# Block-wise first inversion and a regrouping list scheduler in a fused delta-rule, gated-MLP and rotor kernel

## The chip, the cores and the metric

One core of one Trainium2 chip. The metric is the device time of one execution in microseconds, as the median of several. "Before" took 726.74 us (median of 3, 725.66 to 727.87).

Engines by their names in the profile: PE is TensorE's matmul, PEld its weight load, DVE is VectorE, ACT ScalarE, POOL GpSimd, and SP the engine that starts the DMA transfers.

## The reference

Three layers in a row, all in fp32, with 4 batches, 8 heads, 768 tokens and head dimension 48:

```python
for t in range(S):                      # 1: delta rule, per batch and head
    y[:, :, t] = einsum('bhd,bhde->bhe', q[:, :, t], state)
    v_old = einsum('bhde,bhd->bhe', state, kt)          # kt: normalised key
    state = state + bt * einsum('bhd,bhe->bhde', kt, vt - v_old)
...
h = maximum(x @ w_in, 0); u, v = halves of h            # 2: gated MLP
v_n = (v - mean) / sqrt(var + 1e-6)
gated = u * (w_spatial @ v_n + b_spatial);  x = gated @ w_out
...
theta = x @ w_theta; zr, zi = x * cos(theta), x * sin(theta)   # 3: rotor
u = x + w_tok_r @ zr + w_tok_i @ zi;  out = u + maximum(u @ w_ch, 0)
```

## The kernel before

**Chunks.** The recurrence runs in chunks of 64 tokens. 12 chunks make a batch, 48 in all make the chain (0 to 47), and all 8 heads of a chunk run together, two heads side by side on the partitions. Within a chunk the recurrence is a triangular system. Its matrix is inverted beforehand, for 8 chunks (a "round") at a time, so there are 6 rounds; round 0 stands at the start of the program with nothing to hide it.

For each chunk the chain (`chain`) issues on PE, with the line of the profile:
- L875, the read product: keys with the state. DVE subtracts v (L878).
- L887, the update product: the inverted matrix with that difference. ACT or DVE copy it out of PSUM (to U).
- L900, the state product, copied out to S, on which the next chunk's L875 depends.
- L929, the output products, copied to xs and sent through DRAM to layer 2.

Beside them stand the Gram products (`gram2`, L666: keys with keys, two chunks at a time) and the J products (`jit`, L820: keys with queries).

**The inversion** (`invert`). Each 64-row matrix is split into two 32-row diagonal blocks and the block below. DVE transposes (L704), makes norms and factors, scales (L721), and substitutes: 30 steps, each a multiplication (L743) and an addition (L754) over the remaining columns. In round 0 the columns are split in two interleaved sets, so that four instructions belong to one step. Then it scales again (L757) and transposes twice (L761, L763). PE couples the two blocks in two products of 32 rows (L781, L787), with copies in between.

**Layers 2 and 3** are large matmuls (L1040), each fp32 product split into three. V and U (x with w_in), S (w_spatial) and the w_out, theta, y and w_ch products. V, U and S of the first batches run between the products of the chain. What follows the chain is large matmuls alone. The memory for w_out and theta (`p2a`) opens only when all tasks of layer 1 are done.

**The order** is not written out. `Plan` collects tasks with priorities, estimated durations and dependencies, and lists them at build time: at each step the earliest task, and among tasks that could start at once that of the smallest priority. On PE `pe_pick` may choose a large task instead, to keep the clock up, and `filler` (L545) puts idle transposes into gaps. Each engine then runs its list strictly in order.

```python
end, warm, w, acc = self.pe_run(c[1], c[0], c[2], False)
if w > int(c[0] // HAMW) and not warm:
    return best
```

## Time and profile before

| | |
|---|---|
| median of 3 executions | 726.74 us (725.66 to 727.87) |
| the profiled execution | 725.02 us |
| its span, first to last instruction | 722.9 us |
| PE busy | 675.3 us (93%) |
| DVE busy | 560.8 us (78%) |
| ACT busy | 356.3 us (49%) |
| mean granted PE clock, share of full | 0.981 |
| update product of chunk 0, 8 and 47 starts at | 46.76, 110.10, 373.87 us |

The profile is of one execution, and its times count from the span's start. A busy time is the time in which at least one instruction of the engine ran. "Idle" is the rest. A row of the timeline merges like instructions that follow one another: its first column is the start of the first, its second the time to the end of the last. Durations of single instructions overlap their successors; the price of one in a stream is the time from start to start.

### The profile page before, as it was taken

Reading aid. Unit: us, or ns where it says so; the run is one execution under the profiler, and the core shown is the slowest. Engines: PE = TensorE matmul, PEld = TensorE weight load, DVE = VectorE, ACT = ScalarE, POOL = GpSimd, SP = SyncE. Lnnn points to the kernel's source line nnn. Section 1 sums busy time; section 2 is a strip of 40 time slices with the busy share of each in tenths; the row PEclk is TensorE's granted clock in tenths of the full one; section 3 lists DMA queues with packets and bytes.
Section 4 is the critical chain, followed back from the end, with each engine's and each line's share of the span. In section 5 each row is a group of like instructions: output and inputs, shape, how many; then the busy total and the mean of one; then the engine's idle time right before and its main releaser. Section 6 shows DMA issues by size and latency. Waiting matters only on the chain.

```text
span 722.9 us, 23312 instructions
## 1 busy us (share of the span) xinstructions
PE 675.3 (93%) x9750; PEld 619.1 (86%) x9750; DVE 560.8 (78%) x1603; ACT 356.3 (49%) x877; POOL 12.4 (2%) x22
## 2 busy tenths in 40 slices
PE   4585889899999999999999999999999999999997
PEld 4575567688887788878889999999999999999997
DVE  6999989989999989996767868977466745674555
ACT  5756456553369643278646854743244324431331
POOL 0010010010010010010000000000000000000000
PEclk9995899999999999999999999999999999999999
DMA  8544624534567443666778764521111111111001
GB/s 298 172 111 132 201 76 137 145 87 131 171 199 228 125 118 99 188 195 189 241 217 282 222 210 128 162 74 30 66 29 30 30 66 30 30 40 55 1 1 65
DMA packets 74120, 90.62 MB, mean 125 GB/s; under 512 B 7328, under 2 KB 58912, under 8 KB 74016
## 3 DMA queue, kind: packets, MB, share of 16 engines
q1 hardware_dynamic: 74016, 89.14, 40.3%
q8 instruction: 76, 1.25, 0.7%
q14 instruction: 28, 0.23, 0.1%
HBM read 66.70 MB, written 22.41 MB: 123 GB/s over the span
## 4 chain that ended last, share of the span: by engine, by line
PE 54%; DVE 1%; ACT 0%; issue 0%
PE m L1040 29%; PE y L1040 22%; PE m L1351 1%; PE ru L929 1%; PE ru L887 0%; PE ru L875 0%; PE s L900 0%; PE gp L820 0%; PE gp L781 0%; PE gp L787 0%; DVE bgm L964 0%; DVE ul L971 0%; DVE uf L1427 0%; ACT bgr L513 0%; DVE bgm L962 0%
## 5 line engine op out<-in xcount | busy, mean ns | idle before, releaser
L1040 PE MATMUL m<-w,vh 128*128 128x384 f32 x384 | 102.9, 349 | 0.0
L1040 PE MATMUL y<-wr,xTh 128*128 128x384 f32 x432 | 86.9, 338 | 0.0
L1040 PE MATMUL y<-w,xTl 128*128 128x384 f32 x432 | 85.6, 338 | 0.0
L1040 PEld LDWEIGHTS y<-wr,xTh 128*128 128x128 f32 x432 | 75.9, 188 | 0.0
L1040 PEld LDWEIGHTS y<-w,xTl 128*128 128x128 f32 x432 | 75.4, 188 | 0.0
L1040 PEld LDWEIGHTS m<-w,vh 128*128 128x128 f32 x384 | 66.2, 188 | 2.9
L1040 PE MATMUL m<-w,vl 128*128 128x384 f32 x192 | 64.4, 336 | 0.0
L754 DVE TENSOR_TENSOR un<-un,tmp 128x30 f32<-128x30 f32 (+22 forms) x209 | 60.8, 302 | 1.5
L743 DVE TENSOR_TENSOR tmp<-un 128x30 f32<-128x30 f32 (+23 forms) x209 | 60.5, 301 | 1.5
L1376 DVE TENSOR_SCALAR bgr<-m 128x384 int32<-128x384 f32 x22 | 12.3, 558 | 51.1 <-PE m L1040 50.9
L513 ACT ACTIVATE U<-ru 128x96 f32<-128x96 f32 x76 | 15.2, 250 | 63.6 <-PE ru L887 54.3
L1040 PE MATMUL m<-xTh,wih 128*128 128x256 f32 x144 | 44.9, 312 | 1.5 <-ACT hv L513 1.5
L513 ACT ACTIVATE x<-m 128x384 f32<-128x384 f32 x22 | 10.6, 482 | 70.2 <-PE m L1040 70.2
L1040 PE MATMUL m<-wo,gh 128*128 128x384 f32 x176 | 44.7, 334 | 0.0
L1040 PE MATMUL m<-xTl,wih 128*128 128x256 f32 x144 | 40.6, 282 | 0.0
L1040 PE MATMUL m<-xTh,wil 128*128 128x256 f32 x144 | 40.6, 282 | 0.0
L1040 PE MATMUL m<-uh,wc 128*128 128x384 f32 x144 | 38.2, 335 | 0.0
L513 ACT ACTIVATE bgr<-bgr 128x384 uint8<-128x384 uint8 x34 | 36.6, 1075 | 0.5
L1040 PEld LDWEIGHTS m<-w,vl 128*128 128x128 f32 x192 | 36.0, 188 | 0.0
L1040 PE MATMUL m<-wih,xTh 128*128 128x512 f32 x72 | 32.6, 452 | 3.5 <-DVE jp L826 1.2
L1040 PE MATMUL m<-wt,xh 128*128 128x384 f32 x132 | 33.8, 337 | 0.0
L929 PE MATMUL ru<-jp,U 64*64 64x64 f32 x768 | 33.2, 229 | 0.0
(189 smaller groups left out, 1632.6 us busy)
## 6 DMA issues: line engine op xcount, KB each, us to landing
kq<-in_kqT_dram SPq DMA_DIRECT2D x48, 256.0 KB, 3.8
vk<-in_vkn_dram SPq DMA_DIRECT2D x48, 192.0 KB, 2.9
kg<-in_kgT_dram SPq DMA_DIRECT2D x24, 256.0 KB, 3.7
gd<-gt SPq DMA_DIRECT2D x32, 192.0 KB, 3.0
xd<-xs SPq DMA_DIRECT2D x48, 96.0 KB, 2.8
xr<-xd SPq DMA_DIRECT2D x24, 192.0 KB, 3.6
bgr<-in_w_r_dram SPq DMA_DIRECT2D x12, 384.0 KB, 3.8
bgr<-in_w_i_dram SPq DMA_DIRECT2D x12, 384.0 KB, 4.0
```

What stands on the lines that cost most here:

```text
L513: nc.scalar.activation(out=out, in_=in_, func=func, **kw)
L743: nc.vector.tensor_tensor(out=t3, in0=un.t[:, k:k + 1, 0:k].to_broadcast([128, m, k]), in1=un.t[:, t0:32:st, k:k + 1].to_broadcast([128, m ...
L754: nc.vector.tensor_tensor(out=un.t[:, t0:32:st, 0:k], in0=un.t[:, t0:32:st, 0:k], in1=t3, op=ALU.add)
L929: mm(out=PYv[h]()[o:o + 64, c0:c0 + CH], lhsT=lh, rhs=rh, start=f, stop=w == 1 or UF[hp] > 0, skip_group_check=True)
L1040: mm(out=view(), lhsT=a, rhs=c, start=(start and q == 0 and s_ == 0), stop=(stop and q == tot - 1 and s_ == 2))
L1351: nc.tensor.transpose(v3()[:, kk, :], x2.t[:, kk * 128:(kk + 1) * 128], ident.t)
L1376: P.add(o_dve(DM), lambda e: nc.vector.tensor_scalar(out=ni.t.bitcast(I32), in0=th(), scalar1=1.0 / TWO_PI, scalar2=None, op0=ALU.mult), [ ...
```

## The change

Two things at once.

**The first inversion in 16-row blocks** (round 0 only, `I16 = 1`). After the same transpose and factors, DVE substitutes only in the two 16-row diagonal blocks of each 32-row block, both in one instruction, 14 steps. It zeroes the block between them, scales, and makes two transposes (L774, L776). PE joins the 16-row blocks: product A (L793), a combination on DVE (L812), products B (L799) and C (L805), and copies. Then come the coupling products of before (now L725 and L731, in `couple`), in four groups of 8 matrices. The first two groups have priority over chunk 0, the others are placed among the first chunks. The other five rounds substitute as before, but mask and scale with straight writes in place of strided ones.

**The scheduler.** J, later Gram and output tasks become "lazy" (`LZ`, `LZY`, `LZG`): where the choice falls on one, and the task before was not a read or update product, another task that is ready goes first, unless the lazy one's priority is no larger than that of the last such product. `STAY` goes from 0 to 350: while PE runs small products and a large one would be next, a small one that can start within 350 ns goes first. Large V and S tasks are cut into 3 matmuls in place of 6, and constants of the clock estimate and the priorities of the second inversion change. Random priority offsets (`NUDGE`) go away. New memory for y (always in the `ru` bank) and unpadded S and U follow.

```diff
-FILL_LOW = 0.4
-FILL_K = 4
+FILL_LOW = .5
+FILL_K = 16
...
-PER = 6
+PER = 3
...
+LZ = 0.0
+LZY = 0.0
+LZG = 1
+GAPY = 0
+STAY = 350.0
+NUDGE = ()
+SPER = 3
...
-I1P = -8.0
+I1P = 2.5
...
     def pe_pick(self, l, s0, c):
 
+        if c[1].lazy is not None and not self.gap and c[1].prio > self.prog - c[1].lazy:
+            o = [x for x in l if x[1].lazy is None and x[0] <= s0 + 1.0]
+            if o:
+                c = min(o, key=lambda x: (x[1].prio, x[1].uid))
...
+                self.gap = t.gap
+                if t.gap:
+                    self.prog = t.prio
...
+    def invert16(r, pr, gx, G, gg, un, gt, dg, u3, dv, g2):
...
+        for k in range(14, 0, -1):
+            m = 15 - k
+            tmp = r_tmp.new()
...
+                V.tensor_tensor(out=t4, in0=dv()[:, :, k:k + 1, 0:k].to_broadcast([128, 2, m, k]),
+                                in1=dv()[:, :, k + 1:16, k:k + 1].to_broadcast([128, 2, m, k]), op=ALU.mult)
...
+                V.tensor_tensor(out=dv()[:, :, k + 1:16, 0:k], in0=dv()[:, :, k + 1:16, 0:k], in1=t4, op=ALU.add)
...
+        A([("DVE", 1090.0)], lambda e: V.transpose(out=p1.t.rearrange("p u s -> p s u"), in_=u3()[:, :, 0:16].rearrange("p t s -> p s t")),
+          [un], [p1], pr + 0.05, crit=cr, port=False)
+        A([("DVE", 1944.0)], lambda e: V.transpose(out=zt.t.rearrange("p u t -> p t u"), in_=u3()), [un], [zt], pr + 0.1, crit=cr, port=False)
...
+        for h, u0 in enumerate(range(0, 32, MG)):
+            p2 = pr + 0.2 if cr and h == 0 else 8.0 * r + 2.0 * h - (GH if r else HP0)
...
+            def fA(e, u0=u0, va=va):
+                for u in range(MG):
+                    for q in (0, 32, 64, 96):
+                        mm(out=va()[q:q + 32, u, :], lhsT=gx[q:q + 16, u0 + u, 0:32], rhs=p1.t[q:q + 16, u0 + u, :],
+                           start=True, stop=True, tile_position=(q, q))
+
+            def fB(e, u0=u0, vb=vb, cc=cc, vc=vc):
+                for u in range(MG):
+                    for q in (0, 64):
+                        mm(out=vc()[q:q + 32, u, :], lhsT=zt.t[q:q + 32, u0 + u, :], rhs=cc[q:q + 32, u, :],
+                           start=True, stop=True, tile_position=(q, q))
...
+            A(o_dve(16 * MG), lambda e, cc=cc, va=va: V.scalar_tensor_tensor(
+                out=cc[:, :, 0:16], in0=va(), scalar=mask3.t[:, 32:33],
+                in1=mask3.t[:, 0:16].unsqueeze(1).to_broadcast([128, MG, 16]), op0=ALU.mult, op1=ALU.add),
+              [m, mask3], [cb], p2, crit=cr, port=False)
...
+            couple(r, h, u0, MG, p2 + 0.05, gx, G, lambda u, u0=u0, ux=ux: ux.t[:, u - u0, :], [ux], [bx], [bx, bz], ps, o + 256, m2)
...
             A([("DVE", d_dve(1024))], lambda e: nc.vector.tensor_tensor(
-                out=un.t.rearrange("p t u -> p u t"), in0=gx[:, :, 0:32], in1=mask2.t.unsqueeze(1).to_broadcast([128, 32, 32]), op=ALU.mult),
-              G + [mask2, gg[1], gg[3]], [un], pr)
+                out=gx[:, :, 0:32], in0=gx[:, :, 0:32], in1=mask2.t.unsqueeze(1).to_broadcast([128, 32, 32]), op=ALU.mult),
+              G + [mask2, gg[1], gg[3]], gm2, pr)
...
         A([("DVE", d_dve(1024))], lambda e: nc.vector.tensor_tensor(
-            out=gx[:, :, 0:32].rearrange("p s t -> p t s"), in0=un.t, in1=gt.t.unsqueeze(1).to_broadcast([128, 32, 32]), op=ALU.mult),
-          [un, gt] + ub, gg, pr + 0.05, crit=cr)
+            out=u3(), in0=u3(), in1=gt.t.unsqueeze(1).to_broadcast([128, 32, 32]), op=ALU.mult), [un, gt], ub, pr + 0.05, crit=cr)
...
+        elif LZG:
+            mt.lazy = LZ
...
-        A(o_pe(YPE if c else YPE // 2), fy, [kq, jp] + (ss if c else []) + uu, pys + [(xs, True)], pr + YP, act=0.6)
+        A(o_pe(YPE if c else YPE // 2), fy, [kq, jp] + (ss if c else []) + uu, [py, (xs, True)], pr + 0.5, act=1.0)
         ys_b.append(P.tasks[-1])
+        P.tasks[-1].lazy = LZY
```

**What moves, on DVE at the end of the first inversion** (`un` is the matrix, `tmp` the multiplied row, `GX` the 64-row matrices). Before:

```order
L743 TENSOR_TENSOR tmp<-un 128x42 x2
L754 TENSOR_TENSOR un<-un,tmp 128x14x3 x2
L743 TENSOR_TENSOR tmp<-un 128x28
L743 TENSOR_TENSOR tmp<-un 128x30
L754 TENSOR_TENSOR un<-un,tmp 128x14x2
L754 TENSOR_TENSOR un<-un,tmp 128x15x2
L743 TENSOR_TENSOR tmp<-un 128x15 x2
L754 TENSOR_TENSOR un<-un,tmp 128x15 x2
L757 TENSOR_TENSOR GX_121<-un,gaT 128x32x32
L761 STREAM_TRANSPOSE un<-GX_121 128x32x32
L763 STREAM_TRANSPOSE GX_121<-un 128x32x32
```

Now, at the same place:

```order
L763 TENSOR_TENSOR un<-un,tmp 128x2x12x3
L758 TENSOR_TENSOR tmp<-un 128x52
L763 TENSOR_TENSOR un<-un,tmp 128x2x13x2
L758 TENSOR_TENSOR tmp<-un 128x28
L763 TENSOR_TENSOR un<-un,tmp 128x2x14
L771 TENSOR_TENSOR un<-un,gaT 128x2x16x16
L774 STREAM_TRANSPOSE p_583<-un 128x16x32
L776 STREAM_TRANSPOSE uT<-un 128x32x32
L850 TENSOR_TENSOR GX_123<-GX_123,mask_115 128x32x32
L812 SCALAR_TENSOR_TENSOR cc_152<-gp,mask_116 128x8x16
```

Each step has one multiplication and one addition, where it had two of each; the steps go from 14 down, not from 30. L850, the mask of the second inversion, has come up to stand right behind.

**On PE from the first coupling to the update product of chunk 0** (`un`, `ct`, `cc`, `ux`, `uT`, `p` are inputs of the coupling and the join, `ident` the fillers). Before, from the first L781 on:

```order
L781 MATMUL gp<-un,GX_121 32x32 x16
L545 MATMUL ru<-ident 128x128 x15
L787 MATMUL gp<-GX_121,ct 32x32 x16
L820 MATMUL m<-kq 64x64 x8
L545 MATMUL ru<-ident 128x128 x10
L820 MATMUL m<-kq 64x64 x8
L545 MATMUL gp<-ident 128x128
L781 MATMUL gp<-un,GX_121 32x32 x16
L545 MATMUL ru<-ident 128x128
L887 MATMUL ru<-rt,GX_121 64x48 x8
```

Now, from the first C product to chunk 0's update product (L1029); products A and B of the first group stand right ahead of this piece:

```order
L805 MATMUL gp<-uT,cc_152 32x32 x32
L799 MATMUL gp<-cc_153,uT 32x32 x16
L725 MATMUL gp<-ux,GX_122 32x32 x16
L805 MATMUL gp<-uT,cc_153 32x32 x32
L962 MATMUL m<-kq 64x64 x8
L731 MATMUL gp<-GX_122,ct 32x32 x16
L561 MATMUL ru<-ident 128x128
L725 MATMUL gp<-ux,GX_122 32x32 x16
L561 MATMUL ru<-ident 128x128
L962 MATMUL m<-kq 64x64 x8
L561 MATMUL ru<-ident 128x128 x2
L1029 MATMUL ru<-rt,GX_122 64x48 x8
```

Two rounds through the copies (A to B and C, then the coupling) have taken the place of one, and 4 fillers that of 27.

**On PE around the output product of chunk 47** (`w`, `vh`, `vl` are S, `wih`, `wil`, `xTh`, `xTl` are V). Before, the output product (L929) comes 6 matmuls behind the update product:

```order
L887 MATMUL ru<-rt,GX_123 64x48 x8
L1040 MATMUL m<-w_1260,vh 128x384
L1040 MATMUL m<-w_1419,vh 128x384
L1040 MATMUL m<-w_1260,vl 128x384
L1040 MATMUL m<-w_1503,vh 128x384
L1040 MATMUL m<-w_1511,vh 128x384
L1040 MATMUL m<-w_1503,vl 128x384
L929 MATMUL ru<-kq,S_118 64x64 x2
L929 MATMUL ru<-jp,U_120 64x64 x2
```

Now (L1067) it is preceded by V products, and followed by more of them; the update product lies 189 rows of large matmuls ahead:

```order
L1177 MATMUL m<-wil_158,xTh 128x512
L1177 MATMUL m<-wih_155,xTl 128x512
L1177 MATMUL m<-wih_156,xTh 128x512
L1177 MATMUL m<-wil_159,xTh 128x512
L1177 MATMUL m<-wih_156,xTl 128x512
L1067 MATMUL ru<-kq,S_119 48x64 x2
L1067 MATMUL ru<-jp,U_121 48x64 x2
```

It has moved behind work on other batches, and with it the end of layer 1.

## Rows read from the trace of the kernel before

**Rows 1.** Busy time by stage: start:end, length, busy us (instructions), clock, DMA.

```profile
0.00:40.45 40.45, 23.75 (x469) 22.05 (x470) 34.16 (x148) 23.44 (x53) 0.44 (x8) 1.00 0.63 210
46.76:110.10 63.34, 47.07 (x1333) 38.30 (x1332) 59.06 (x183) 37.57 (x110) 1.93 (x2) 0.81 0.50 146
110.10:373.87 263.77, 253.33 (x5738) 212.59 (x5737) 234.76 (x724) 146.14 (x399) 7.98 (x8) 0.99 0.55 163
373.87:722.90 349.03, 344.81 (x2059) 340.74 (x2058) 227.20 (x536) 146.47 (x311) 0.14 (x2) 1.00 0.27 84
```

**Rows 2.** Timeline of DVE, first inversion: start, us, engine line op.

```profile
9.76 1.92 DVE L704 STREAM_TRANSPOSE un<-GX 128x1024 f32<-128x1024 f32 x1 [0.16 <-ACT GX L513]
...
14.10 1.23 DVE L721 TENSOR_TENSOR un<-un,gaT 128x1024 f32<-128x1024 f32 x1
...
15.62 0.28 DVE L743 TENSOR_TENSOR tmp<-un 128x30 f32<-128x30 f32 x2
...
25.00 0.47 DVE L743 TENSOR_TENSOR tmp<-un 128x120 f32<-128x120 f32 x2
25.39 0.47 DVE L754 TENSOR_TENSOR un<-un,tmp 128x120 f32<-128x120 f32 x2
...
38.95 1.25 DVE L763 STREAM_TRANSPOSE GX<-un 128x1024 f32<-128x1024 f32 x1
```

**Rows 3.** Timeline of DVE, end of the second substitution.

```profile
90.39 0.27 DVE L754 TENSOR_TENSOR un<-un,tmp 128x108 f32<-128x108 f32 x1
90.69 0.24 DVE L743 TENSOR_TENSOR tmp<-un 128x84 f32<-128x84 f32 x1
...
91.90 0.21 DVE L743 TENSOR_TENSOR tmp<-un 128x30 f32<-128x30 f32 x1
92.15 0.22 DVE L754 TENSOR_TENSOR un<-un,tmp 128x30 f32<-128x30 f32 x1
```

**Rows 4.** Groups on DVE by form: busy us, mean ns | idle before.

```profile
L761 DVE STREAM_TRANSPOSE un<-GX 128x1024 f32<-128x1024 f32 x6 | 12.1, 2024 | 0.1
L757 DVE TENSOR_TENSOR GX<-un,gaT 128x1024 f32<-128x1024 f32 x6 | 12.0, 2000 | 0.1
...
L721 DVE TENSOR_TENSOR un<-un,gaT 128x1024 f32<-128x1024 f32 x6 | 7.3, 1218 | 0.1
```

**Rows 5.** Timeline of PE, update, state and output products, first w_out.

```profile
46.76 0.45 PE L887 MATMUL ru<-rt,GX 64*64 64x48 f32 x16
...
110.10 0.45 PE L887 MATMUL ru<-rt,GX 64*64 64x48 f32 x16
...
111.30 0.52 PE L900 MATMUL s<-U,vk 64*48 64x48 f32 x16 [0.51 <-ACT U L513]
...
375.50 0.27 PE L929 MATMUL ru<-kq,S 48*64 48x64 f32 x2
...
396.06 0.51 PE L1040 MATMUL y<-wo,gh 128*128 128x384 f32 x2
```

**Rows 6.** Busy time around the second inversion, and at the lower clock.

```profile
40.20:96.54 56.34, 41.75 (x1101) 34.11 (x1099) 53.86 (x176) 31.44 (x96) 1.89 (x2) 0.79 0.52 154
...
57.00:79.60 22.60, 15.52 (x361) 12.63 (x361) 21.81 (x82) 11.34 (x37) 0.00 (x0) 0.50 0.53 156
```

**Rows 7.** Timeline of PE, from large to small products.

```profile
92.58 0.28 PE L1040 MATMUL m<-xTl,wih 128*128 128x256 f32 x1
92.69 0.28 PE L1040 MATMUL m<-xTh,wil 128*128 128x256 f32 x1
92.90 0.40 PE L900 MATMUL s<-U,vk 64*48 64x48 f32 x16
```

**Rows 8.** Timeline of PE, V products of 512 columns.

```profile
384.21 0.39 PE L1040 MATMUL m<-wih,xTh 128*128 128x512 f32 x1
384.44 0.39 PE L1040 MATMUL m<-wil,xTh 128*128 128x512 f32 x1
```

**Rows 9.** Timeline of DVE, the last part of w_out.

```profile
399.14 0.55 DVE L971 TENSOR_TENSOR wo<-cvm,wo 128x384 fp32r<-128x384 f32 x1
```

More of the change, by code (lines that the diff above doesn't have):

```diff
@@ L114 @@
 WEARLY = 1
+I16 = 1
+BK16 = 12
+MG = 8
+HP0 = 1.8
+GH = 1.0
 SLX = 0.0
@@ L155 @@
 class Task:
-    __slots__ = ("opts", "fn", "deps", "prio", "extra", "crit", "users", "left", "eng", "start", "end", "allocs", "uid", "big", "act", "credit", "order", "banks", "port", "part", "mode", "slack")
+    __slots__ = ("opts", "fn", "deps", "prio", "extra", "crit", "users", "left", "eng", "start", "end", "allocs", "uid", "big", "act", "credit", "order", "banks", "port", "part", "mode", "slack", "lazy", "gap")
 class PEFILL:
@@ L588 @@
     PSb = [Buf(tile_=PSt) for _ in range(2)]
+    r_y, PYv = r_ru, [RUt[:, h, 256:448] for h in range(2)]
+    RUz = Buf(tile_=RUt)
     for b_ in PSb:
@@ L620 @@
     load(mask2, lambda: mask2.t, mask2_c, 16384, -21.2)
+    load(mask3, lambda: mask3.t, mask3_c, 16896, -21.1)
+    CC = [pools["pa"].tile([128, MG, 32], F32, name=f"cc{i}") for i in range(2)]
+    ccb = [Buf(tile_=x) for x in CC]
+    for i in range(2):
+        A([("POOL", 450.0)], lambda e, i=i: nc.gpsimd.tensor_copy(CC[i], mask3.t[:, 0:32].unsqueeze(1).to_broadcast([128, MG, 32])),
+          [mask3], [ccb[i]], -20.0, port=False)
     for q in (32, 96):
         A([("DVE", 300.0)], lambda e, q=q: nc.vector.memset(PSt[q:q + 32, :, 0:2 * D], 0.0), (), PSb, -31, port=False, part=q)
-    for i in range(2):
-        A([("POOL", 100.0)], lambda e, i=i: nc.gpsimd.memset(St[i][:, HP * D:], 0.0), (), SS[i], -30 + i, port=False)
-        A([("POOL", 100.0)], lambda e, i=i: nc.gpsimd.memset(Ut[i][:, HP * D:], 0.0), (), UU[i], -30 + i, port=False)
+        A([("DVE", 600.0)], lambda e, q=q: nc.vector.memset(RUt[q:q + 32, :, 256:448], 0.0), (), [RUz], -31, port=False, part=q)
     kq_b, vk_b, jp_b = {}, {}, {}
@@ L680, in gram2, with couple, f2, f3 @@
                 A(o_cpp(256), lambda e, w=w, gxj=gxj: copy(e, gxj, pvs[w]()), [pss[w]], [G], pr, port=False)
+    def couple(r, h, u0, mu, p2, gx, G, xf, xr, x3, x4, ps=None, o=256, pb=None):
+        cr = r == 0
+        if ps is None:
+            ps = pb = r_gp.new()
+        ct = r_ct.new()
+        pv = GPt[:, o:o + mu * 32].rearrange("p (a b) -> p a b", b=32)
+        def f2(e):
+            for u in range(mu):
+                for q in (0, 64):
+                    mm(out=pv[q + 32:q + 64, u, :], lhsT=gx[q:q + 32, u0 + u, 32:64], rhs=xf(u0 + u)[q:q + 32],
+                       start=True, stop=True, tile_position=(q, q + 32))
+        def f3(e):
+            for u in range(mu):
+                for q in (0, 64):
+                    mm(out=pv[q:q + 32, u, :], lhsT=ct.t[q + 32:q + 64, u, :], rhs=gx[q + 32:q + 64, u0 + u, 32:64],
+                       start=True, stop=True, tile_position=(q + 32, q))
+        A(o_pe(525 * mu // 8), f2, xr + G[u0 // HP:(u0 + mu) // HP], [(ps, True), (pb, pb is ps)], p2, crit=cr, act=0.38, mode=3)
+        P.tasks[-1].order.update(seqs[-1:])
+        seqs.append(P.tasks[-1])
+        for q in (1, 3):
+            A(o_cpp(32 * mu), lambda e, q=q: copy(e, ct.t[32 * q:32 * q + 32, 0:mu], pv[32 * q:32 * q + 32]),
+              [pb], [(ct, True)], p2, crit=cr, port=False, part=32 * q)
+            ps.readers.append(P.tasks[-1])
+        A(o_pe(525 * mu // 8), f3, [ct] + x3, [(ps, True), (pb, True)], p2, crit=cr, act=0.46, mode=3)
+        for q in (0, 2):
+            A(o_cpp(32 * mu), lambda e, q=q: copy(e, gx[32 * q:32 * q + 32, u0:u0 + mu, 32:64], pv[32 * q:32 * q + 32]),
+              [pb] + x4, [G[i] for i in range(u0 // HP, (u0 + mu) // HP)], p2, crit=cr, port=False, part=32 * q)
+            ps.readers.append(P.tasks[-1])
@@ L823, in jit @@
             jp = jp_b[g] = r_jp.new()
-            A(o_pe(JPE), f, [kq_b[g]], pss + [jp], pr, after=grams if r < 2 else (), act=0.55)
+            A(o_pe(JPE), f, [kq_b[g]], pss + [jp], pr, after=grams if r < 2 else (), act=0.75).lazy = LZ
             for h in (0, 1):
@@ L830, in jit @@
             jp = jp_b[g] = jp_b[g + 1] = r_jp.new()
-            A(o_pe(2 * JPE), f, [kq_b[g], kq_b[g + 1]], pss + [jp], pr, after=grams if r < 2 else (), act=0.55)
+            A(o_pe(2 * JPE), f, [kq_b[g], kq_b[g + 1]], pss + [jp], pr, after=grams if r < 2 else (), act=0.75).lazy = LZ
             A(o_dve(512), lambda e: nc.vector.tensor_tensor(
@@ L899, in fs @@
                         i = 64 - a if UF[hp] else a
[L900 removed]
+                        mm(out=at(PSt, SB[hp])[a:a + D], lhsT=v.t[i:i + 64, 1, hp, :], rhs=u[i:i + 64, UB[hp], :],
                            start=f, stop=l, skip_group_check=True)
[L903 removed]
+            A(o_pe(SPE), fs, [v] + uu, PSb, pr, crit=True, act=0.81)
             for h in (0, 1):
[L905 to L911 removed]
+                A(o_cpp(96), lambda e, h=h: copy(e, two(sn)[0:112, h], PSt[0:112, h, 0:2 * D]), [PSb[h]], [ssn[h]], pr, crit=True, port=False)
+        py = r_y.new()
         yc = (lambda w, hp: (w, 64 * (SB[hp] % 2)) if UF[hp] else (YF[hp], 128))
```

190 lines of the change are left out of this document (116 added, 74 removed).

## The prediction

> **What bounds the kernel now.** I read the busy time by stage first, then the timelines of PE and DVE where the stages meet, and the order of the instructions on PE and DVE before and after. A chunk is 64 tokens of one batch, counted 0 to 47; "product 8" is the update product (L887) of chunk 8. Four stages are to be seen in [rows 1]. Until 40.45 us nothing can start, since the first inversion runs on DVE: PE's 23.75 us of busy time there are Gram products and fillers. From product 0 to product 8 (46.76 to 110.1 us, 63.3 us) DVE is the bound: 59.06 busy against PE's 47.07, at a mean clock of 0.81. From product 8 to product 47 (263.8 us) PE is: 253.33 busy, so 10.4 idle. After product 47 PE is alone on the path, 344.81 of 349.03.
>
> So I ask two things: how much earlier product 8 comes, and whether PE has more or less to do after it. By the order, PE has passed the same 63 large matmuls at product 8 before and now, and the same 2745 stand behind it.
>
> **The first inversion.** Before, DVE starts it at 9.76, scales at 14.10, substitutes from 15.62 to about 34.9 in 118 instructions, and ends the last transpose at 40.20 (38.95 + 1.25) [rows 2]. Now only the two 16-row diagonal blocks are substituted, in 28 instructions of 28 to 112 elements, each of which needs the one before it. Before, two interleaved halves of the columns kept the instructions apart: four of 120 elements start 0.39 us per pair, 0.195 each (25.00, 25.39) [rows 2]. The price of dependent ones stands where the second inversion ends: 0.30 us from start to start at 108 elements, 0.25 at 30 [rows 3]. With these 28 instructions cost 14 x 0.26 (28 to 72) + 14 x 0.30 (88 to 112) = 7.8 us. Their bounds are 28 x 0.195 = 5.5 and 28 x 0.30 = 8.4; I take 7.8, since the rows are of this very code. In the Trainium skill, "VectorE: DVE Perf Modes", section "The DRAIN you can't avoid", chained instructions cost no more than unchained ones, because each waits for the pipeline to empty anyway. The rows disagree (0.30 against 0.195 at about the same size); by that rule the substitution would take 5.5, and the forecast would be 2.3 lower.
>
> The rest goes by [rows 2, 4]. From the first transpose to the scaling stays 4.34. Scaling half of the elements: half of 1.22, 0.6, and the diagonal 0.1. Second scaling of the half: 0.6. A transpose that writes with a stride costs 2.02, half of one 1.0, so the two new ones 3.0. Sum: 9.76 + 4.34 + 0.7 + 7.8 + 0.6 + 3.0 = 26.2; with the one instruction of chunk 0 in between (0.3) and handoffs I take 26.9. That is 13.3 us before 40.20.
>
> The join is new: 320 matmuls of 32 rows, 4 combining instructions on DVE and 40 copies out of PSUM of a quarter of the partitions. Half of it stands ahead of product 0, half among chunks 1 to 4. From the end of DVE's part to product 0 it was 6.6 us (40.20 to 46.76) [rows 2, 5]. Now one more round through PE, a copy and PE again stands there: between 6.6 and twice that, product 0 at 33.5 to 40.1. I take 36, nearer to the one round, as the two first groups run into each other.
>
> **From there to product 8.** Chunk 0 early is worth nothing by itself: chunk 8 is the first that needs the second inversion, and that is DVE's. Before, from 40.20 to its last transpose at 96.54 DVE had 56.34 us and was busy for 53.86 of them [rows 6]. By the order it now has 195 instructions between these two marks, and had 175. The second inversion itself gets cheaper: masking and scaling with straight writes, 1.22 each where strided ones took 2.00 [rows 4], while its first transpose now reads across, 1.92 in place of the 1.25 of a straight one [rows 2]: 0.9 saved. The 20 more are for the most part copies, casts and combinings of 96 to 256 columns; at 0.21, near the lower of the small instructions' 0.195 and 0.30 [rows 2, 3], 4.2. Net +3.3. So the mark moves to 26.9 + 56.3 + 3.3 = 86.5, 10.0 us earlier, and with the same 13.6 us behind it product 8 to 100.1. Bounds: all handoffs of the join on DVE's path (+4, as it waits for the copies' sources in its queue) and none of the added work on it (-3).
>
> In this stretch the granted clock was 0.50, the level of 1.2 GHz, from 57.0 to 79.6, with PE busy 15.52 of 22.60 and DVE 21.81 [rows 6]: DVE sets the pace there, so I give a drop there no price, and none to the join's 160 later matmuls, which lie in PE's 16 us of idle time.
>
> **The scheduler, after product 8.** Large, Gram, state and output products are the same in number; 8 more J products and 5 fewer fillers cancel. Changes between small and large products fall from 247 to 231. One costs 0.10: from one 256-wide matmul to the next 0.11, to the first small one 0.21 [rows 7]. That is -1.6; with the fillers -2.0 at most, and I take -2.0. Against it: between a chunk's products PE has less to do while it waits for the copies. By the order 15 of 36 places between the update product (L887) and the state product (L900) have less than 1.0 us of other work on PE, before 7; between the read product (L875) and the update product 12 of 37, before 11. Such a place idled 0.51 at chunk 8 [rows 5]. Most are covered to 0.7 us, so I take +1.0 (between 0 and 27 x 0.51 = 13.8, the upper end being a rival below).
>
> **The seam to the last stage.** The output product of chunk 47 is now "lazy": it stands not a microsecond but some 39 us behind product 47, and that frees the memory into which w_out is loaded. Before, from that product (375.50) to the last part of w_out ready (399.14 + 0.55) it was 24.2 us [rows 5, 9], with the first products of w_out at 396.06 on its other parts. Now 90 large matmuls stand between, 63 of 256 columns at 0.11 to 0.12 [rows 7] and 27 of 512 at 0.23 [rows 8], 13.7 us; with the product itself (0.6) and 9 matmuls that need only the other parts (1.6), the last part is wanted after 16.0. PE works in order and waits for it: at most 24.2 - 16.0 = 8.2. In the sync queue that part's load now stands ahead of a store, another load and a weight, some 6 us of the 24.2, so I take 2.5.
>
> **Sum.** -10.0 - 2.0 + 1.0 + 2.5 = -8.5 us. The profiled execution took 725.02 us (span 722.9), the median shown is 726.74, 1.7 more: 716.5 against the first, 718.2 against the second.
>
> **Rivals.**
> A. DVE's relief goes on. All five later inversions lose 0.9 us of DVE work, and DVE was busy for 234.76 of the 263.77 us in which PE idled 10.4 [rows 1]. If 7 of these 10.4 go and the seam and the thinner covers cost nothing: -10.0 - 2.0 - 7 = 19 less, 708. For it: DVE is near full there. Against: PE is fuller still.
> B. The change does not do what it says: the join eats the gain. If each of its four groups waits for DVE and ACT queues as the pair ahead of product 0 did (6.6 us), product 0 comes at 40, the copies push the second inversion, and product 8 comes 3 us earlier, not 10: 725. For it: DVE is 95% busy there and takes copies. Against: half the groups have room among chunks that DVE paces anyway.
> C. Slower: the answers of ACT and DVE between a chunk's products are late. Place: the 27 thinly covered places of product 8 to 47; price up to 0.51 each, 13.8, all on PE's path: -8.5 + 12.8, some 731. It decides from 0.4 each (10.7 us make the change slower by 0.3%). For it: fewer covers, DVE 89% busy. Against: 18 such places existed, and PE idled only 10.4 us in the whole stage.
>
> **Chances.** Forecast 0.58, its own range 713 to 723; A 0.14, B 0.16, C 0.12. About 0.3%, 2.2 us, is what a measurement of this kernel can tell from no change. Faster: forecast and A, and a third of B, 0.77; within 0.3%: the rest of B, 0.11; slower: C, 0.12. The range from 707 to 728 leaves out the far ends of A and C.
>
> **What would show it.** The last of DVE's first-inversion transposes ends at about 27; dependent steps 0.25 to 0.30 apart. Product 0 at about 36, the second inversion's last transpose at about 86.5, product 8 at about 100. From product 8 to the end it was 612.8; the forecast says 614, and 623 would mean that all that was won ahead is lost there. At the seam PE should wait some 2.5 us for w_out. If product 8 comes at 107, B holds; if PE idles over 20 us between products 8 and 47 on ACT's and DVE's copies, C.

## The result, and the profile after

The changed kernel took 735.08 us (median of 4 runs, 732.40 to 740.08), the kernel before 726.63 in the same session (725.66 to 727.87): a ratio of 1.0123, 95% interval 1.0074 to 1.0173. It is slower, by 8.5 us, where 8.5 us less had been forecast. The profiled execution took 732.40 us (span 730.6).

| | before | forecast | after |
|---|---|---|---|
| DVE's part of the first inversion ends | 40.20 | 26.9 | 27.73 |
| product 0 | 46.76 | 36 | 46.41 |
| second inversion's last transpose starts | 96.54 | 86.5 | 104.20 |
| product 8 | 110.10 | 100.1 | 119.62 |
| product 8 to the end of the span | 612.8 | 614 | 611.0 |

So the error lies ahead of product 8: 19.5 us, of which the 3.0 behind it give back a part. Busy time by stage, as in [rows 1] (stage, length, busy us of PE, PEld, DVE, ACT, POOL, granted clock, DMA):

```profile
0.00:46.41 46.41, 31.12 (x861) 27.13 (x861) 28.38 (x84) 22.83 (x56) 2.16 (x10) 0.87 0.59 190
46.41:119.62 73.21, 60.68 (x1691) 49.98 (x1691) 61.80 (x197) 44.44 (x123) 3.11 (x6) 0.67 0.43 122
119.62:364.73 245.11, 236.02 (x5675) 196.40 (x5669) 223.13 (x691) 141.96 (x403) 8.06 (x8) 1.00 0.56 167
364.73:730.60 365.87, 359.98 (x2137) 355.09 (x2136) 234.24 (x552) 152.69 (x321) 0.14 (x2) 0.99 0.28 87
```

From product 8 to product 47 PE idles 9.1 us, a little less than before. From product 0 to product 8 no engine is full any more: DVE is busy for 61.80 of 73.21, PE for 60.68, at a mean clock of 0.67. The timeline of DVE, with the rows that answer to [rows 2, 6] first and then two waits:

```profile
25.75 1.98 DVE L776 STREAM_TRANSPOSE uT<-un 128x1024 f32<-128x1024 f32 x1
...
31.61 0.35 DVE L812 SCALAR_TENSOR_TENSOR cc<-gp,mask 128x128 f32<-128x128 f32 x1 [0.27 <-PE gp L799]
...
37.61 0.41 DVE L535 COPY ux<-gp 32x256 f32<-32x256 f32 x1 [3.84 <-ACT GX L529]
...
104.20 1.25 DVE L931 STREAM_TRANSPOSE GX<-un 128x1024 f32<-128x1024 f32 x1
```

DVE ends its part at 27.73 (25.75 + 1.98) and then waits for the join. Up to the second inversion's last transpose ("the transpose" from here on) it has 8.4 us less to do than before, and still gets there 7.7 us later. Busy time up to that mark, of the kernel before:

```profile
0.00:96.54 96.54, 65.25 (x1567) 56.07 (x1567) 87.81 (x323) 54.88 (x149) 2.33 (x10) 0.88 0.57 178
```

and of the changed kernel:

```profile
0.00:104.20 104.20, 77.65 (x2191) 66.00 (x2192) 79.39 (x256) 59.16 (x161) 3.37 (x14) 0.74 0.54 164
```

DVE idled 8.7 us before and idles 24.8 now, 18.0 of them ahead of product 0. The join itself, on PE (L793 product A, L799 B, L805 C, L725 and L731 coupling, L1029 update product; in brackets the idle time ahead and what ended it, where "issue" means that the profile shows nothing that PE waited for):

```profile
28.74 1.39 PE L793 MATMUL gp<-p,GX 16*32 16x16 f32 x128
30.79 0.69 PE L799 MATMUL gp<-cc,uT 32*32 32x32 f32 x32 [0.67 <-DVE cc L812]
32.01 0.50 PE L805 MATMUL gp<-uT,cc 32*32 32x32 f32 x34 [0.52 <-DVE cc L812]
33.16 0.45 PE L805 MATMUL gp<-uT,cc 32*32 32x32 f32 x30 [0.65 <-issue]
34.56 1.07 PE L799 MATMUL gp<-cc,uT 32*32 32x32 f32 x32 [0.96 <-ACT ux L529]
36.09 1.06 PE L725 MATMUL gp<-ux,GX 32*32 32x32 f32 x32 [0.46 <-ACT GX L529]
...
42.11 1.07 PE L731 MATMUL gp<-GX,ct 32*32 32x32 f32 x32 [1.84 <-ACT GX L529]
...
46.41 0.68 PE L1029 MATMUL ru<-rt,GX 64*64 64x48 f32 x16
...
55.07 0.46 PE L1029 MATMUL ru<-rt,GX 64*64 64x48 f32 x7 [1.70 <-issue]
```

Read the waits against what the products need. B of the second group (34.56) needs only its own combining step, which was done at 31.96; it waits for ACT's copy `ux` of the first group. That copy needs only B of the first group (done at 31.48) and starts after C. The copy of the first group's C (`GX`), which was done at 33.61, starts only when B of the second group is done (35.63). Both on ACT:

```profile
33.66 0.76 ACT L529 ACTIVATE ux<-gp 32x256 f32<-32x256 f32 x2 [2.62 <-PE gp L805]
35.67 0.37 ACT L529 ACTIVATE GX<-gp 32x256 f32<-32x256 f32 x1 [1.25 <-PE gp L799]
```

All of them use one PSUM tile, `gp`, into which PE's products write and from which DVE and ACT copy, the first group in columns 0 to 511, the second in 512 to 1023. As these rows show them, the program's waits go by the tile and not by the columns: whoever writes it waits for those who read it, and the reverse. Products and copies of both groups take turns, and the join takes 18.7 us where PE works on it for 8.7. And the clock falls to 0.50, the level of 1.2 GHz, after 6 us in which PE did these products of 16 and 32 columns with waits between them (3.75 busy):

```profile
28.00:34.00 6.00, 3.75 (x231) 3.03 (x229) 3.89 (x13) 3.32 (x9) 1.22 (x4) 1.00 0.45 131
34.00:36.00 2.00, 1.07 (x32) 0.96 (x32) 0.00 (x0) 0.74 (x3) 0.00 (x0) 0.50 0.89 233
36.00:76.00 40.00, 29.62 (x873) 24.33 (x873) 27.08 (x99) 21.41 (x63) 1.22 (x4) 0.50 0.32 89
```

Before, it was 0.50 from 57.0 to 79.6 only [rows 6]. The next place to see is between products 4 and 5, 16.7 us apart (before 5.8), on PE:

```profile
76.03 0.68 PE L1029 MATMUL ru<-rt,GX 64*64 64x48 f32 x16
...
80.71 0.69 PE L725 MATMUL gp<-ux,GX 32*32 32x32 f32 x32 [0.85 <-ACT ux L529]
...
84.44 0.45 PE L1017 MATMUL ru<-S,kq 48*64 48x48 f32 x16
...
88.09 0.26 PE L1067 MATMUL ru<-kq,S 48*48 48x64 f32 x2 [2.31 <-DVE rt L1020]
...
92.70 0.68 PE L1029 MATMUL ru<-rt,GX 64*64 64x48 f32 x16
...
106.16 0.45 PE L1029 MATMUL ru<-rt,GX 64*64 64x48 f32 x16
...
119.62 0.45 PE L1029 MATMUL ru<-rt,GX 64*64 64x48 f32 x16
```

The join's last group (here its coupling, L725) stands ahead of the read product of chunk 5 (L1017). That is half of the gap; behind the read product PE waits 2.31 us for DVE, and output and Gram products stand ahead of product 5. At the seam to the last stage, the wait of PE between 360 and 425 us:

```profile
PE m L1177 <- DVE mv L1224: 2.2, 1, 2.2
```

### The profile page after: what moved, and what is told of

The parts are those of the page before. It is cut to its first block, busy times and chain, and to the rows that moved or that the text cites. A ratio compares the mean times of both kernels' runs of the same rounds, so it can differ in the third digit from the quotient of the medians.

```text
span 730.6 us, 24523 instructions
## 1 busy us (share of the span) xinstructions
PE 687.8 (94%) x10356; PEld 628.6 (86%) x10356; DVE 547.5 (75%) x1523; ACT 361.9 (50%) x900; POOL 13.5 (2%) x26
## 5 line engine op out<-in xcount | busy, mean ns | idle before, releaser
L1513 DVE TENSOR_SCALAR bgr<-m 128x384 int32<-128x384 f32 x22 | 12.3, 558 | 56.4 <-PE m L1177 56.3
L911 DVE TENSOR_TENSOR tmp<-un 128x30 f32<-128x30 f32 (+9 forms) x150 | 49.0, 327 | 1.1
L922 DVE TENSOR_TENSOR un<-un,tmp 128x30 f32<-128x30 f32 (+9 forms) x150 | 49.0, 327 | 1.0
L1177 PE MATMUL m<-xTh,wih 128*128 128x256 f32 x144 | 44.4, 308 | 1.7 <-ACT hv L529 1.6
L529 ACT ACTIVATE x<-m 128x384 f32<-128x384 f32 x22 | 10.6, 482 | 67.5 <-PE m L1177 67.5
L529 ACT ACTIVATE GX<-gp 128x256 f32<-128x256 f32 (+2 forms) x74 | 30.3, 428 | 22.1 <-PE gp L696 8.2
L529 ACT ACTIVATE gh<-graw 128x256 fp32r<-128x256 f32 x25 | 9.2, 413 | 49.9 <-PE m L1177 49.9
```

Of the source, the lines that this page charges most:

```text
L529: nc.scalar.activation(out=out, in_=in_, func=func, **kw)
L911: nc.vector.tensor_tensor(out=t3, in0=u3()[:, k:k + 1, 0:k].to_broadcast([128, m, k]), in1=u3()[:, t0:32:st, k:k + 1].to_broadcast([128, m ...
L922: nc.vector.tensor_tensor(out=u3()[:, t0:32:st, 0:k], in0=u3()[:, t0:32:st, 0:k], in1=t3, op=ALU.add)
L1177: mm(out=view(), lhsT=a, rhs=c, start=(start and q == 0 and s_ == 0), stop=(stop and q == tot - 1 and s_ == 2))
L1513: P.add(o_dve(DM), lambda e: nc.vector.tensor_scalar(out=ni.t.bitcast(I32), in0=th(), scalar1=1.0 / TWO_PI, scalar2=None, op0=ALU.mult), [ ...
```

## The experiments

Each kernel was timed beside the kernel before. "DVE part" is where DVE's part of the first inversion ends, "transpose" the start of the second inversion's last transpose, "behind" the time from product 8 to the end of the span, all from one profiled execution; the last column is the ratio to before with its 95% interval.

| kernel | DVE part | product 0 | transpose | product 8 | behind | median us | ratio |
|---|---|---|---|---|---|---|---|
| before | 40.20 | 46.76 | 96.54 | 110.10 | 612.8 | 726.6 | 1 |
| changed | 27.73 | 46.41 | 104.20 | 119.62 | 611.0 | 735.1 | 1.0123 (1.0074 to 1.0173) |
| scheduler alone | 41.58 | 47.7 | 105.33 | 115.19 | | 737.1 | 1.0112 (1.0068 to 1.0156) |
| inversion alone | 28.04 | 48.0 | 83.66 | 115.46 | 624.9 | 748.9 | 1.0298 (1.0255 to 1.0340) |
| second group's own tile | 28.40 | 44.4 | 104.65 | 113.9 | 624.4 | 739.3 | 1.0153 (1.0095 to 1.0211) |
| fillers in the join | 28.41 | 47.7 | 105.51 | 117.2 | 613.1 | 732.1 | 1.0077 (1.0043 to 1.0111) |
| groups one by one | 30.10 | 43.18 | 95.49 | 113.69 | 614.9 | 728.6 | 1.0025 (0.9995 to 1.0055) |
| one by one, two tiles | 27.82 | 39.43 | 91.74 | 109.87 | 613.7 | 727.5 | 1.0009 (0.9989 to 1.0028) |
| later groups earlier | 29.02 | 40.87 | 98.40 | 113.41 | 615.0 | 727.0 | 1.0006 (0.9989 to 1.0022) |
| later groups without A, B, C | 29.64 | 41.38 | 96.03 | 106.90 | 625.7 | 736.1 | 1.0151 (1.0111 to 1.0192) |
| two tiles in all groups | 28.48 | 39.07 | 90.91 | 107.59 | 618.7 | 726.5 | 0.9996 (0.9979 to 1.0013) |
| fillers up to product 7 | 29.04 | 40.39 | 102.68 | 122.50 | 614.1 | 737.1 | 1.0129 (1.0081 to 1.0178) |
| no fillers up to product 8 | 28.32 | 40.06 | 91.36 | 112.26 | 614.7 | 727.4 | 0.9995 (0.9967 to 1.0023) |
| before without shifts | 40.52 | 46.45 | 95.76 | 109.33 | 622.1 | 733.6 | 1.0092 (1.0071 to 1.0112) |
| two tiles, shifts, late | 28.78 | 40.87 | 93.19 | 109.89 | 606.2 | 718.3 | 0.9878 (0.9844 to 0.9911) |
| two tiles, shifts, middle | 28.64 | 40.53 | 101.91 | 111.64 | 616.3 | 731.3 | 1.0059 (1.0039 to 1.0080) |

The profiled execution of the scheduler alone lies 9 us above its median, so its last stage is not given; that of the inversion alone lies 7 below its median.

**Which half of the change costs.** The scheduler alone:

```
-I16 = 1
+I16 = 0
```

> The changed kernel with its first inversion put back to 30 steps over 32 rows and one coupling, as before; the scheduler's new numbers and rules stay. If the join is what cost the time, product 0 stands at about 46.5 us as before, product 8 near 110 against 119.6, and from product 8 to the end about 611 us as in the changed kernel, so 722 to 724 us, below the 726.6 of before. If the scheduler's part is to blame (its numbers starve TensorE early), product 8 stays near 118 and the time stays above 731.

The inversion alone (the numbers of several lines stand on one; the planner's other constants also go back, the random shifts do not):

```
-FILL_LOW = .5    FILL_K = 16   PER = 3   SPER = 3   ...
+FILL_LOW = .4    FILL_K = 4    PER = 6   SPER = 6   ...
-LZ = 0.0    LZY = 0.0    LZG = 1   STAY = 350.0   I1P = 2.5
+LZ = None   LZY = None   LZG = 0   STAY = 0.0     I1P = -8.0
...
```

> The changed kernel with the scheduler's part undone (fill share 0.4 and 4, groups of 6, activity levels and weights as before, no late products, no staying with small ones, second inversion's rank -8); the 16-row inversion and its join stay. If the join costs the time, product 0 stands at 45 to 47 us, product 8 at 115 to 120, and with 613 us after it the time is 730 to 735. If the scheduler's part is to blame, product 0 stands at 40 or earlier, product 8 near 102 to 105 and the time near 717 to 720.

My theory was the join, my rival the scheduler. By what I had written, the first run speaks for the scheduler (737.1 us, above 731) and the second for the join (product 0 at 48.0, product 8 at 115.46). Each half is slower than before by itself, and in both the random shifts of before are missing as well (below). The scheduler alone has product 8 at 115.19, 5.1 later than before, as the second inversion comes 8.8 us later. I put that down to its rank, 2.5 now and -8 before, but no run changes the rank alone. From product 0 to the transpose, of before, of the scheduler alone and of the changed kernel:

```profile
46.76:96.54 49.78, 35.19 (x944) 28.55 (x943) 48.05 (x160) 28.80 (x91) 0.00 (x0) 0.76 0.57 168
```

```profile
47.74:105.33 57.59, 47.97 (x1163) 39.30 (x1158) 53.32 (x176) 33.48 (x100) 0.00 (x0) 0.79 0.57 166
```

```profile
46.41:104.20 57.79, 46.53 (x1331) 38.87 (x1332) 51.02 (x173) 36.34 (x106) 1.22 (x4) 0.63 0.50 143
```

This stretch is as long without the join as with it. Without it DVE is busy for 53.32 us, 5.3 more than before: other work now stands ahead of the second inversion. The inversion alone has the transpose 12.9 us earlier than before, as DVE's relief promised, and still has product 8 at 115.46: the join holds product 0 at 48.0, and products 4 and 5 are 14.4 us apart (79.1, 93.5). So there the join costs more than the relief brings, and there is a second cause behind product 8 (below).

**Turns on one tile, or the clock.** The second group in another tile, in unchanged order up to product 0:

```
-va = (lambda o=o: GPt[:, o:o + 16 * MG] ...
+va = (lambda o=o, ti=ti: (PSt[:, 0, 128:128 + 16 * MG] if ti else GPt[:, o:o + 16 * MG]) ...
...
+            ti, TC = (r == 0 and h == 1), None
```

> The changed kernel, with the second eight columns of the first join (their products A, B, C and their coupling) written to a PSUM tile of their own (free columns of the state's tile) and not to the tile of the first eight; TensorE's instructions up to product 0 keep their order. If the shared tile makes the steps take turns, the two groups now overlap: product 0 at 40 to 42 us against 46.4, and the time 729 to 732 against 735. If the halved clock alone makes the join long, product 0 stays at 45 to 46.5 and the time at 734 to 736.

Fillers behind the join's products:

```
 def fC(e, u0=u0, vb=vb, cc=cc, h=h):
...
+                if cr and h < 2:
+                    filler((5, 8)[h], "ru")
```

> The changed kernel with 35 filler transposes more, put behind the products of the first join (3 to 8 behind each), so that TensorE works while it waits for the copies; nothing else moves. If the fallen clock is the cause, the granted clock stays at 1.00 up to product 0, the products of the join take 0.69 us and not 1.06, product 0 comes at 43.5 to 44.5 us, and the time falls to 730 to 732. If the turns through the shared tile are the cause, product 0 stays within 1 us of 46.4 and the time at 734 to 736.

Both fell short. With its own tile for the second group product 0 comes at 44.4, 2.0 earlier and not 4 to 6, and the time is 739.3, not 729 to 732. DVE's part does not end at the same time in each execution (28.40 here, 27.73 in the changed kernel), so the join is best counted from there: 16.0 us, 2.7 less. PE's timeline there has two waits that no engine ends:

```profile
34.12 0.41 PE L808 MATMUL gp<-uT,cc 32*32 32x32 f32 x28 [2.10 <-issue]
...
38.95 0.64 PE L808 MATMUL s<-uT,cc 32*32 32x32 f32 x30 [1.68 <-issue]
```

Together they are 3.8 us, where the changed kernel's join has 0.8 of that kind (0.65 and 0.17), so the turns between the two groups may be worth more than 2.7.

With fillers the clock is back at 0.93 from 40 to 52 us (0.50 without), and the coupling products there take 0.69 again; from 34 to 40 us it is at 0.56. Product 0 is not earlier but 1.3 later (the join takes 19.3): the fillers stand in PE's queue. Product 8 is 2.4 earlier and the time 3 us less, which is what the clock theory gave for the total, but not by its path, and the two ratios' intervals overlap. So this run does not show that the halved clock makes the join long; nor does it rule that out, as the clock was back only from 40 us on and the fillers take time of PE themselves.

**One group at a time, then two tiles.** In the first, the second group's product A is put behind the first group's last coupling product; in the second, B and the coupling of the first group also write another tile than A and C:

```
+            ta.order.update(seq3[-1:] if cr else ())
```

> The changed kernel, with the groups of eight columns of the first join one after the other: the first product of a group stands behind the last coupling product of the group before it, so only the first group lies ahead of product 0. If the join is long because its steps take turns on one PSUM tile, so that every step of the second group delays the first, product 0 comes 6 to 8 us earlier, at 38 to 40 us, and the second group's turns lie behind it; product 8 at 108 to 114 and the time 725 to 731. If the halved clock makes it long, product 0 stays at 44 to 46 and the time at 734 to 736.

```
+            ti, TC = (r == 0 and h == 0), None
+            if ti:
+                TC = PSt[:, 1, 128:384]
-            vc = (lambda o=o: GPt[:, o + 256:o + 256 + 32 * MG] ...
+            vc = (lambda o=o, ti=ti: (PSt[:, 1, 128:128 + 32 * MG] if ti else GPt[:, o + 256:o + 256 + 32 * MG]) ...
```

> As the kernel with one group after the other, and in the first group the products B and the coupling write another PSUM tile (free columns of the state's tile) than A and C. If turns on the shared tile are what the join waits for, product 0 comes earlier once more, at 35.5 to 37.5 us, which is where the prediction had it; otherwise it stays within 0.5 us of the kernel with one group after the other. The order behind product 0 is the same in both, so product 8 and the time should move by no more than product 0 does: 723 to 730 us.

Product 0 goes from 46.41 to 43.18 and on to 39.43, the transpose from 104.20 to 95.49 and 91.74, product 8 from 119.62 to 113.69 and 109.87, and the time from 1.0123 to 1.0025 and 1.0009 of before. But the second step is smaller than it looks, as the first of these kernels started its join late: ahead of the substitution DVE waited 3.55 us for a square root on ACT, 0.98 in the changed kernel. That wait there, and the end of DVE's part with the second group's own tile, with one group at a time, and with two tiles:

```profile
15.84 0.35 DVE L871 RECIPROCAL nT<-sr 128x32 f32<-128x32 f32 x1 [3.55 <-ACT sr L529]
```

```profile
26.43 1.97 DVE L776 STREAM_TRANSPOSE uT<-un 128x1024 f32<-128x1024 f32 x1
```

```profile
28.16 1.94 DVE L777 STREAM_TRANSPOSE uT<-un 128x1024 f32<-128x1024 f32 x1
```

```profile
25.88 1.94 DVE L777 STREAM_TRANSPOSE uT<-un 128x1024 f32<-128x1024 f32 x1
```

Counted from the end of DVE's part the join takes 18.7 us in the changed kernel, 13.1 with one group at a time and 11.6 with two tiles (10.6 to 12.1 in the seven other kernels with two tiles); 9.1 had been predicted. So putting the second group behind product 0 is worth 5.6 us. That takes its turns away, but its own products and copies too, and the mean clock in the join rises with it (0.67 to 0.85); the kernel with the second group's own tile puts 2.7 on the turns. The second tile is worth 1.0 to 2.5 more, by one execution against eight, and the times of the two kernels, 728.6 and 727.5, do not differ beyond their intervals. With two tiles DVE idles 15.5 us up to the transpose (91.74 less 76.23 busy) and not 24.8. PE with two tiles:

```profile
34.17 0.53 PE L725 MATMUL s<-ux,GX 32*32 32x32 f32 x22 [1.32 <-issue]
...
39.10 0.40 PE L797 MATMUL gp<-p,GX 16*32 16x16 f32 x14 [0.47 <-issue]
39.43 0.68 PE L1034 MATMUL ru<-rt,GX 64*64 64x48 f32 x16
```

Of the 2.5 us above the predicted 9.1, 1.8 are again waits for nothing that is shown. Product 0 is 3 to 5 us later than I expected of the first kernel, and 2 to 4 of the second.

**The later groups.** Three kernels on top of that one: ranks two higher (`HP0 = 3.8`), the later groups' A, B and C left out, and the second tile for every group (`ti = r == 0`; there the later groups write into the tile in which the state sums up, and the output is no longer that of the reference).

> As the kernel with one group after the other and two PSUM tiles in the first, with the rank of the later groups raised by 2 (they stand one chunk earlier in the order). If the gap of 16.7 us between products 4 and 5 comes from the last group's steps standing there, it falls to 5 to 8 us, product 8 comes at 102 to 108 us and the time is 718 to 726 us; if it comes from VectorE's second inversion, the gap moves to products 7 and 8, product 8 stays at 113 or later, and the time at 729 or more.

> As the kernel with one group after the other and two PSUM tiles in the first, but the second, third and fourth group leave out their products A, B and C, the copies behind these and the diagonal factor: only the coupling products stay (so the output lacks these blocks). If the later groups' steps between the products are what keeps the chain and VectorE waiting, products 0 to 7 follow each other in 6 to 7 us (9.2 on average with the groups), VectorE idles less than 11 us up to the second inversion's last transpose, which comes at 84 to 88 us, and product 8 at 97 to 102. If the halved clock alone stretches the stage, the products keep 8 to 9 us each and product 8 stays at 107 or later. The order behind product 8 is another one, so the total says little: 715 to 735.

```
+            if cr and h:
+                couple(r, h, u0, MG, p2 + 0.05, gx, G, lambda u: zt.t[:, u, :], [zt], [], [], None, 256)
+                continue
```

> As the kernel with one group after the other and two PSUM tiles in the first group, but now every one of the four groups has its B and coupling in the second tile; the order stays. If turns on the shared tile still delay the later groups, products 1 to 6 follow each other about 1 us faster, product 8 comes at 104 to 108 (109.9 with two tiles in the first group alone) and the time is 721 to 726. If the state's copies, which now share that tile, take the turns in their place, product 8 stays at 109 to 113 and the time at 726 to 730.

Without A, B and C in the later groups the products do follow each other in 6.3 us (41.38 to 85.48 for seven, 9.2 with them), as expected; but the transpose comes at 96.03, not at 84 to 88, and product 8 at 106.90, not at 97 to 102. PE:

```profile
85.48 0.45 PE L1037 MATMUL ru<-rt,GX 64*64 64x48 f32 x16
...
106.90 0.68 PE L1037 MATMUL ru<-rt,GX 64*64 64x48 f32 x16
```

So product 8 waits for two chains, the products 0 to 7 and the second inversion, and only the later one counts. Here the first is early and the second is not; DVE is busy for 79.22 us up to the transpose, 3.0 more than with the groups, so it does more of other work first. Two tiles in all groups bring product 8 another 2.3 earlier (107.59), as expected at the late end, but not the time (726.5); the order with earlier groups moves the gap to products 1 to 4 and product 8 back to 113.41. Neither of these two moves the time from that of before by more than its interval. The kernel without A, B and C is 1.5% slower, by what lies behind product 8 (625.7), where its order is another one.

**What the halved clock costs between products 0 and 8.** Twelve fillers behind each state product of chunks 0 to 6 and six in the join, to hold the clock, and the opposite, none of the planner's 16 fillers there:

```
+                if g < 7:
+                    filler(12, "ru")
```

> As the kernel with one group after the other and two PSUM tiles in the first, with 6 filler transposes more behind C of the first group and 12 behind the state product of each of chunks 0 to 6, in an unchanged order. If the halved clock (0.50 from about 34 to 84 us) stretches the stage, it now stays near 1.00 there, and product 8 comes 3 to 6 us earlier, at 104 to 107, and the time is 721 to 725. If it costs nothing there, because the waits for the copies set the pace, product 8 stays at 109 to 112 with a granted clock near 1.00, and the time at 726 to 730.

```
+        if 0 in marks and marks[0].end is not None and marks[8].end is None:
+            return
```

> As the kernel with one group after the other and two PSUM tiles in the first, without the 16 filler transposes that stand between products 0 and 8 (11 of them, 2.61 us at the halved clock, ahead of product 6). If TensorE's own queue, slowed by the halved clock, paces products 0 to 8, product 8 comes 2 to 4 us earlier, at 106 to 108 us, and the time falls to 723.5 to 726. If waits for copies and VectorE pace them, the fillers fill waits, product 8 stays at 109 to 111 and the time at 727 to 728.

The first did not hold the clock (0.50 from 40 to 64), so it does not answer its question; it shows another thing. PE spends 20.66 us on fillers between products 0 and 8 where it spent 4.45, and that stretch takes 82.1 us where it took 70.4: of 16.2 us more in PE's queue, 11.7 come out at product 8. The second answers it for one stretch, though product 8 came as neither of its two cases had it: it is 2.4 later (112.26), and the time is the same (727.4). Without the 11 fillers (2.61 us) product 6 comes 2.6 us earlier, 92.80 against 95.42, or 3.3 counted from product 0; and then the clock, at 1.00 from 86 to 90 us, falls to 0.50. The stretch from product 6 to product 7 with two tiles and the fillers, and without them:

```profile
95.42:104.07 8.65, 8.65 (x288) 7.21 (x287) 4.88 (x12) 5.27 (x13) 0.87 (x1) 0.95 0.23 58
```

```profile
92.80:106.47 13.67, 13.67 (x290) 11.16 (x287) 6.33 (x17) 7.77 (x17) 2.11 (x2) 0.53 0.18 49
```

The same products, PE full in both, 8.65 us at a clock of 0.95 and 13.67 at 0.53. Here the halved clock costs 5.0 us, twice what the fillers cost that bring it back. In the changed kernel the same stage ends so: from 108 to 117 us PE is busy for 8.57 of 9.00 at 0.62.

**What lies behind product 8.** The kernel before without its four random shifts of ranks, and the two-tile kernel with one new draw, late (with a shorter stay and more lead) or in the middle:

```
-NUDGE = ((9376, 863, 1113, 0.3), (6411, 2108, 2228, 0.6), (938, 2559, 2679, 0.6), (1081, 1922, 2422, 0.3))
+NUDGE = ()
```

> The kernel before with its four random shifts of ranks taken out (they touch tasks from the third inversion on and move nothing ahead of product 26). If the order that the shifts were picked for is worth something, as the changed kernel has none, this kernel is slower than before with an unchanged product 8 (110 us): 730 to 735 us. If the shifts are worth nothing, 725 to 728 us.

```
-NUDGE = ()   STAY = 350.0   LGI = 5
+NUDGE = ((1976, 2800, 2900, 0.6),)   STAY = 200.0   LGI = 6
```

> As the kernel with one group after the other and two PSUM tiles in the first, with the random shifts that the change dropped put back in another draw (one range of late tasks), a shorter stay with small products (200) and one more chunk of lead for the later rounds. Up to product 12 the order is the same, so product 8 stays at 109 to 111. If the order of the late work is worth what the shifts of before were (9.3 us behind product 8), 611 to 615 us behind product 8 become 605 to 609 and the time is 719 to 723; if such shifts are worth nothing here, it stays at 726 to 729.

```
-NUDGE = ()
+NUDGE = ((8803, 1400, 1600, 0.2),)
```

> As the kernel with one group after the other and two PSUM tiles in the first, with one draw of random shifts in the middle of the list and nothing else; it brings the later groups of the join and products 1 to 7 closer together in the order. If the gaps between products 4 and 8 are a matter of the order, product 7 comes at 88 to 96 us (104.1) and product 8 at 102 to 107, and the time is 719 to 724. If the halved clock and the turns set them, product 8 stays at 109 or later and the time at 726 or more.

Busy time up to product 8 and behind it, of the kernel before without shifts:

```profile
0.00:109.33 109.33, 76.23 (x1957) 65.03 (x1957) 98.91 (x346) 63.63 (x168) 4.30 (x12) 0.89 0.53 166
109.33:731.40 622.07, 602.25 (x7784) 556.08 (x7783) 462.00 (x1250) 294.58 (x718) 8.33 (x10) 0.99 0.38 117
```

and of the two-tile kernel with a late draw:

```profile
0.00:109.89 109.89, 87.67 (x2585) 76.47 (x2585) 89.27 (x285) 71.39 (x186) 5.61 (x16) 0.77 0.54 163
109.89:716.10 606.21, 598.09 (x7794) 554.91 (x7793) 451.59 (x1229) 295.60 (x726) 7.73 (x10) 1.00 0.40 120
```

The shifts of before are worth 9.3 us behind product 8 (612.8 against 622.1) and 6.9 us of the time, and nothing ahead of it. The change dropped them; the rest of it makes that good and a little more (611.0). With a late draw and two more numbers the two-tile kernel takes 718.3 us and beats both: 1.2% faster than before, 2.3% than the changed one (718.3 / 735.1). How much of that is the draw and how much the two numbers, no run separates. The draw in the middle brought product 7 to 97.9 (104.1 without it, 88 to 96 expected), but the transpose to 101.91, and the time to 731.3: a draw is no sure gain.

## Why the prediction was wrong

It was wrong in its sign, and the step that failed is the join: "Now one more round through PE, a copy and PE again stands there: between 6.6 and twice that, product 0 at 33.5 to 40.1." It was 18.7 us, above the upper bound of 13.2. I counted rounds that the data need and did not look at which PSUM tile they go through: "the two first groups run into each other" does not hold, they take turns. A second step failed beside it: the scheduler has no term of its own ahead of product 8 (the sum has only 20 more instructions on DVE there), and alone it makes product 8 5.1 us later than before. Point by point, the 19.5 us at product 8:

- DVE's part of the first inversion: right. The 28 dependent steps took 7.87 us (16.12 to 23.99; 7.8 predicted, and not the 5.5 of the lower bound), the end was 27.73 (26.9): +0.8.
- The join: +9.6. With only one group ahead of product 0 it is 5.6 less, with two tiles 7.1. Turns on one tile are shown for 2.7 between the groups (the second group's own tile, all else in place; one execution, where the kernels with two tiles scatter by 1.5) and for 1.0 to 2.5 within the first group (two tiles). What else is in the 5.6, more turns, the second group's own work or the lower clock, no run separates. Of the 2.5 left, 1.8 are waits that the profile names only "issue".
- Product 0 to the transpose: 57.8 and not 50.5, +7.3. "So the mark moves to 26.9 + 56.3 + 3.3" took DVE for the bound because it had been 95% busy. From the end of its part to the transpose it was to be busy for 57.2 of 59.6 us; it was busy for 58.8 of 76.5. So the work was sized right, and the waits, 17.6 us for 2.5, were not: 10.9 fall into the join, 6.8 behind product 0. But the scheduler alone takes 57.6 from product 0 to the transpose without a join, so the new order on DVE has its part in this term. With one group ahead of product 0 and two tiles it took 52.3, 1.8 above the forecast.
- From there to product 8: 15.4 and not 13.6, +1.8. "I give a drop there no price" was wrong, and the clock is the likely reason here: it is at 0.78 and was at 1.00, with PE busy for 14.15 of the 15.4. A low clock was free as long as DVE paced the stage, and here DVE does not. The kernel without fillers shows the price where PE leads, 5.0 us in one such stretch; in the changed kernel it is argued, not shown. How much of the changed kernel's 73.2 us the clock costs in all is open: no run held it at 1.00 there with nothing else changed.
- Behind product 8: 611.0 where 614 was said, so the size was right, but not the terms. The price of dropping the random shifts, 9.3 us, was not in the sum, and what the rest of the change gains there, some 11, stood there as 2.0 less 1.0. That the two cancel was luck.
- The seam: 2.2 us of wait, 2.5 predicted, but not for w_out: PE waits for the layer norm of the last V products (`mv`, L1224).

Of the rivals, C did not happen: PE idles 9.1 us between products 8 and 47, not over 20. B had the mechanism, the join's steps waiting for ACT and DVE, with product 0 at 40 and product 8 still 3 us ahead; it was larger than B made it. A did not show.

## What to carry to other kernels

Before you price a chain of small products and copies, write down for each step not only the data it needs but the PSUM tile that it writes, and who else reads or writes that tile; in this program steps on one tile took turns, however many columns lay between them. An engine that is 95% busy is the bound only while nothing new makes it wait: when work is taken from it, price the waits that the replacement adds, and the low clock of the other engine that had cost nothing behind it. Before you subtract two marks of two profiles, look whether the piece began at the same time: here one wait on ACT moved the start of the join by 2.4 us and made a second step look larger than it was. And when a change drops numbers that were drawn at random for the old order, time the old kernel without them first; here that alone was 6.9 us.

## What the runs showed of the hardware

TensorE stopped for 0.65 to 2.10 us in the middle of products of 32 x 32, with nothing that the profile shows to wait for (0.65 in the changed kernel, 2.10 and 1.68 with the second group's own tile, 1.32 with two tiles). It is not a matter of that shape: in the changed kernel it stopped for 1.70 in the middle of the update product of chunk 1 (64 x 48). The cause stays open. Fillers cost most of their own time where PE paces (11.7 us for 16.2 of them), and paid for it only where they brought the clock back (2.6 us for 5.0). I had expected that the waits leave room for them and that they keep the clock near 1.00; it was 0.50 from 40 to 64.
